# Sliding-window attention into a hard-swish product: unpadded casts, 64x64 transposes and one Q/K copy for batches 0 and 1

## The chip, the cores and the metric

The kernel runs on one core of a Trainium2 chip. The metric is device time of one execution in microseconds (us); of several runs the median is given. Engines: PE is TensorE (PEld its weight loads), DVE is VectorE, ACT is ScalarE, POOL is GpSimd, SP is SyncE, which issues the DMAs here.

## The reference

```
q, k, v: (8 batches, 8 heads, 576, 64); w_in (512, 2048); w_out (2048, 512); all float32
scores = (q @ k^T) / 8, kept where 0 <= i - j < 64, else -1e9
attn   = softmax(scores) ; o = attn @ v
x = o with heads side by side: (4608, 512)
h = x @ w_in ; g = h * clip(h + 3, 0, 6) / 6 ; out = g @ w_out
```

## The kernel before

**Tiling.** Attention goes by batch b and pair of heads g (0 to 3, two heads of 64 make 128 partitions). Its output, transposed, is xT. The second half goes by token block T of 512 tokens, nine of them: `s1(T)` (L620) multiplies xT with w_in (L641, 64 products of 512 columns a block, in most blocks each in two parts), ACT and DVE form g (L650, L653), and `s2(T)` (L661) multiplies with w_out (L685, 64 products), ACT copies the result out (L702) and SP stores it (L705). Attention of batch T+1 is placed between the L685 of `s2(T)`. Batch 0 comes ahead of everything.

**One pair of heads.** The scores of a 128-key block are needed for 192 queries only (QW). `scores` (L510) makes five key blocks for two heads: ten products (L530) on 64-row tiles of PE, one row half for each head. For batch 0 a product with a table of -30000 (L523) masks first; for later batches DVE multiplies by a 0/1 mask after the exponential (L550). ACT takes the exponential (L539, L545). `pv` (L558) is 18 products (L567, L572) with V, which has a column of ones for the sum; DVE divides (L582, L585). `xt` (L605) transposes the result on PE for batches 0 and 1 (L609) and ACT copies it to xT (L616); from batch 2 on a DMA transpose does (L592).

**Q and K.** From batch 2 on (`load_nat`, L362) POOL casts q and k to bf16, and one DMA transpose each (L371) makes QT and KT. For batches 0 and 1 (`load_pairs`, L296; `tq`, L486) a partition holds nine consecutive rows of one head. A load brings 64 partitions of one head and 64 of the other. Two casts of 64 partitions each write into a zero-padded tile (`padded`), with the second head in the upper columns. Nine products with `fold`, two 64x64 identities stacked (L500), give the transpose of one of Q and K for both heads, in f32. Two copies, 320 columns by DVE (L261) and 256 by ACT (L263), put rows back in order (L505). The copy and cast functions share the lines L261, L263 and L264 (one for each engine), so the profile tells them apart by tile name.

**Order.** All is put into order by a planner (`Plan`, L34) while the program is built: each engine's instructions come in the order of planned times. It holds a clock for PE (`pl.t`), booked costs for operations (`DUR`, `PER_COL`), a time for each engine's becoming free, and for DMA a running time `dma["t"]` that grows by kilobytes over a rate and lands 1.9 us later (`moved`, L253). The engine of each operation is fixed in tables (`ENG_CAST`, `ENG_TR`, L356). Batch 0's units are taken when `ready` (L459) says so, by `PRIO`. Batch 1's units are in the list `FIRST` (L748); at each L685 of `s2(0)` the head of the list is taken if the planner believes its inputs to have been ready for 0.3 us (L673). A unit placed too early holds everything behind it on PE.

Loads go out on SP in one sequence (`load_items`, L270): batch 0's q, k and V in two halves, w_in, w_out, batch 1's q and k, its V, then q, k and V of each later batch. Each load waits for a staging slot (`stage_slot`, six of them) and for its destination; the next one waits behind it.

```
                while side and side[0][0] <= n:
                    at_, f, b, g = side[0]
                    if b < NR6 and not ready(f, b, g):
                        break
```

Of the kernel before, what the change touches and what calls it, by code (L numbers as in the profile page):

```python
# [21 lines left out]
NQT = 1  # L22
NPT = 3
NNP = 4
NXP = 2
NEG = -30000.0
NWARM = 11
ENG_TR = ((("DVE", "ACT"), ("DVE", "ACT")), (("DVE", "ACT"), ("DVE", "ACT")))
DUR = lambda eng, n: {"DVE": 0.156 + 1.04e-3 * n, "ACT": 0.165 + 0.83e-3 * n}[eng]
PRIO = lambda g, f: ({"S": 0, "tq": 1, "tk": 1, "PV": 2, "X": 3}[f], g)  # L30
PAD_OF = ((0, 1, 0, 1), (2, 3, 0, 1))


class Plan:  # L34

# [20 lines left out]
    def pop(self):  # L56
        it = heapq.heappop(self.heap)
        ready, _, eng, dur, fn, key, then, deps = it
        for d in deps:
            if d not in self.done:  # L60
                self.parked.setdefault(d, []).append(it)
                return
            if self.done[d] > ready:
                heapq.heappush(self.heap, (self.done[d],) + it[1:])
                return
        start = max(ready, self.free.get(eng, 0.0))
# [32 lines left out]
def kernel(  # L99
# [18 lines left out]
    R = 9  # L118
# [48 lines left out]
    fold = consts.tile([P, NP], BF16, name="fold")  # L167
# [10 lines left out]
    padded = [[consts.tile([P, R, P], BF16, name=f"pad{i}{j}") for j in range(NNP)] for i in range(2)]  # L178
    natural = [consts.tile([P, NG, KB, P], BF16, name=f"nat{i}") for i in range(2)]
    QK_ring = [[consts.tile([P, NG, SP], BF16, name=f"{n}T{i}") for n in "QK"] for i in range(NQT)]  # L180
# [5 lines left out]
    for i in range(2):  # L186
        r = slice(i * NP, (i + 1) * NP)
        nc.vector.tensor_copy(out=fold[r, :], in_=ident32[r, r])
# [6 lines left out]

    for j in range(NNP):
        for i in range(2):
            for hf in range(2):
                r = slice((1 - hf) * NP, (2 - hf) * NP)
                eng, dur = "DVE", 0.3  # L200
                at(eng, (0.0, 0.0, 20.0, 20.0)[j], dur, zero(eng, padded[i][j][r, :, hf * D : (hf + 1) * D]),
                   ("pad", i, j) if hf else None)
    for pair in QK_ring:
        for t in pair:
            at("DVE", 4.5, 0.2, zero("DVE", t[:, :, S:SP]))
    at("DVE", 3.0, 0.25, lambda: nc.vector.tensor_copy(out=ident[:], in_=ident32[:]))
    at("DVE", 14.0, 0.06, lambda: nc.vector.memset(half[:], 0.5))
    for j, t in enumerate(P_ring):
        at("ACT", 1.9, 0.55, lambda t=t: nc.scalar.copy(
            out=t[:, :, 0 : KB - 1, QW : 2 * P], in_=idle[:].rearrange("p (h k w) -> p h k w", h=2, w=D)))  # L210
        at("ACT", 1.9, 0.4, lambda t=t: nc.scalar.copy(
            out=t[:, :, KB - 1, P : 2 * P], in_=idle[:, 0 : 2 * P].rearrange("p (h w) -> p h w", h=2)))

    def band(t, fill):
# [16 lines left out]
        out=neg[:, 2 * QW : TB], in_=neg32[:, 0:P]) and None, "neg", deps=("neg32",))  # L231
# [4 lines left out]
    ) and None, "mask", deps=("mask32",))  # L236
# [7 lines left out]
    dma = {"t": 2.0}  # L244
# [14 lines left out]
    def cast_op(eng, out_ap, in_ap):  # L259
        if eng == "DVE":  # L260
            return lambda s: nc.vector.tensor_copy(out=out_ap, in_=in_ap) and None  # L261
        if eng == "ACT":
# [3 lines left out]
    PER_COL = {"POOL": 0.83, "DVE": 0.45, "ACT": 0.83}  # L266
    ENG_CAST = ([(("DVE", "POOL"), ("ACT", "POOL"))] * 2 + [(("DVE", "POOL"), ("POOL", "POOL"))] * 2,
                [(("ACT", "POOL"), ("DVE", "POOL"))] * 4)
# [11 lines left out]
    def casts(key, land, pieces):  # L280
# [6 lines left out]
        for eng, o_ap, i_ap, cols in pieces:  # L287
            pl.op(eng, land, (0.3 if eng == "DVE" else 0.18) + PER_COL[eng] * cols / 1e3, cast_op(eng, o_ap, i_ap), None, one)

# [6 lines left out]
    def load_pairs(b):  # L296

        vs = load_v(b)
        for gg in range(0, NG, 2):
            tiles = {}  # L300
            deps = [stage_slot([("cast", b, i, gg), ("cast", b, i, gg + 1)]) for i in range(2)]
            for g in (gg, gg + 1):
                for i, src in enumerate((q, k)):
                    def go(s, g=g, i=i, src=src, tiles=tiles):
                        if i not in tiles:
# [6 lines left out]
                        fr, land = moved(s, 295, 380)  # L312
                        n = padded[i][PAD_OF[b][g]]
                        sv = st.rearrange("p (j d) -> p j d", j=R)
                        engs = ENG_CAST[b][g][i]
                        casts(("cast", b, i, g), land, [
                            (engs[1], n[NP:P, :, D:P], sv[NP:P], 576),
                            (engs[0], n[0:NP, :, 0:D], sv[0:NP], 576)])
                        return fr
                    before = [(bb, gg) for bb in range(b + 1) for gg in range(NG)  # L320
                              if (bb, gg) < (b, g) and PAD_OF[bb][gg] == PAD_OF[b][g]]
# [473 lines left out]
```

## Time and profile before

| | us |
|---|---|
| median of 11 runs | 320.22 |
| lowest and highest run | 319.14, 321.99 |
| the profiled execution | 319.55 |
| its span | 317.8 |
| PE busy | 300.2 |
| first L641 (w_in product of block 0) | 23.80 |
| first L641 of block 1 | 65.32 |

Times inside the profile count from the span's start. A line of a timeline has a start, a length, the engine, the line of the code, operation and tiles (written <- read), and how many in a row. "Idle before" names what ended the engine's wait. A matmul's length includes its way through the array, so a row of matmuls is read by their starts. The clock is the share of full speed that PE was granted.

### The profile page before, as it was taken

The numbers are of one execution on the slowest core, as the hardware profiler recorded it, in microseconds if no ns is written. First come the engines' busy times: TensorE is split into PE (matmuls) and PEld (weight loads), VectorE is DVE, ScalarE is ACT, GpSimd is POOL, SyncE is SP. The second block draws the span as 40 slices with busy tenths as digits, with TensorE's granted clock in tenths as the row PEclk, the third lists the DMA queues.
The fourth block names the chain that finished last, engine by engine and source line by source line (L and its number), as shares of the span: only waits on it lengthen the run. The fifth ranks groups of instructions, "written<-read, shape, count | busy, mean of one in ns | idle before, by whom it ended". The sixth has DMA issues, their size and how long they took to land.

```text
span 317.8 us, 5918 instructions
## 1 busy us (share of the span) xinstructions
PE 300.2 (94%) x2348; PEld 158.6 (50%) x2387; DVE 175.6 (55%) x216; ACT 174.9 (55%) x243; POOL 104.0 (33%) x153
## 2 busy tenths in 40 slices
PE   6769779999999999999999999999999999999995
PEld 2544345644454445785544454445575644444442
DVE  7686486637762676267717671777166717404610
ACT  5865368646834683368346833684368426315611
POOL 6787786622610265015601650067003000000000
PEclk9999979999999999999999999999999999999999
DMA  8999999999979899999999999999993430020011
GB/s 221 280 387 385 389 275 199 230 221 228 214 112 204 201 206 200 189 221 192 220 171 231 195 207 193 219 203 201 205 200 54 116 103 0 21 80 34 0 66 68
DMA packets 152812, 58.33 MB, mean 184 GB/s; under 512 B 142032, under 2 KB 142032, under 8 KB 152784
## 3 DMA queue, kind: packets, MB, share of 16 engines
q1 hardware_dynamic: 152784, 57.95, 83.0%
q8 instruction: 19, 0.31, 0.4%
q14 instruction: 9, 0.07, 0.1%
HBM read 36.70 MB, written 9.44 MB: 145 GB/s over the span
## 4 chain that ended last, share of the span: by engine, by line
PE 85%; DMA 8%; DVE 3%; ACT 1%; issue 1%; POOL 1%; POOLq 0%; ACTq 0%
PE acc L685 39%; PE ps L641 35%; DMA st<-in_moe_w_out_dram 5%; PE ps L530 4%; DMA st<-in_moe_w_in_dram 3%; PE ps L567 3%; PE ps L572 2%; PE ps L500 1%; DVE pad L261 1%; DVE pad L191 1%; POOL wout L264 1%; ACT pT L539 0%; POOL pad L264 0%; DVE gT L653 0%; PE ps L609 0%
## 5 line engine op out<-in xcount | busy, mean ns | idle before, releaser
L653 DVE SCALAR_TENSOR_TENSOR gT<-t,ps 128x1024 bf16<-128x1024 bf16 x72 | 87.9, 1221 | 94.2 <-ACT t L650 94.2
L685 PE MATMUL acc<-wout,gT 128*128 128x512 bf16 x551 | 132.5, 382 | 1.4 <-issue 0.3
L641 PE MATMUL ps<-xT,win 128*128 128x512 bf16 (+4 forms) x693 | 125.7, 340 | 0.7
L650 ACT ACTIVATE t<-ps,half 128x1024 bf16<-128x1024 f32 x72 | 80.2, 1114 | 47.5 <-PE ps L641 46.9
L641 PEld LDWEIGHTS <-win 128*128 128x128 bf16 x704 | 65.2, 98 | 59.8 <-issue 0.4
L685 PEld LDWEIGHTS <-gT 128*128 128x128 bf16 x576 | 53.1, 98 | 57.7 <-issue 0.5
L702 ACT COPY osb<-acc 128x512 f32<-128x512 f32 x36 | 21.2, 590 | 70.0 <-PE acc L685 68.8
L539 ACT ACTIVATE pT<-ps 128x768 bf16<-128x768 f32 x64 | 48.6, 817 | 10.1 <-PE ps L530 9.8
L264 POOL CAST V<-st 128x512 bf16<-128x512 f32 (+1 forms) x32 | 19.3, 606 | 103.3 <-DMA st<-in_v_dram 100.1
L264 POOL CAST nat<-st 128x512 bf16<-128x512 f32 x48 | 37.4, 783 | 20.4 <-DMA st<-in_q_dram 10.1
L550 DVE TENSOR_TENSOR pT<-pT,mask 128x1920 bf16<-128x1920 bf16 x28 | 35.3, 1261 | 8.0 <-ACT pT L545 8.0
L585 DVE TENSOR_TENSOR opg<-ps,rec 128x640 bf16<-128x640 f32 x32 | 26.4, 824 | 1.1
L567 PE MATMUL ps<-V,pT 128*128 128x65 bf16 x320 | 22.4, 194 | 3.4 <-ACT pT L539 2.0
L567 PEld LDWEIGHTS <-pT 128*128 128x128 bf16 x320 | 20.5, 98 | 9.1 <-ACT pT L539 2.5
L572 PE MATMUL ps<-V,pT 128*128 128x65 bf16 x256 | 21.3, 194 | 0.0
L530 PE MATMUL ps<-QT,KT 64*128 64x192 bf16 (+1 forms) x320 | 17.9, 239 | 1.0 <-ACT KT L263 0.4
L530 PEld LDWEIGHTS <-KT 64*128 64x128 bf16 x320 | 11.6, 94 | 14.0 <-issue 10.0
L572 PEld LDWEIGHTS <-pT 128*128 128x128 bf16 x256 | 17.9, 97 | 0.0
L582 DVE RECIPROCAL rec<-ps 128x10 f32<-128x10 f32 x32 | 6.9, 216 | 12.8 <-PE ps L572 12.8
L545 ACT ACTIVATE pT<-ps 128x256 bf16<-128x256 f32 x32 | 12.9, 402 | 0.0
L264 POOL CAST pad<-st 64x576 bf16<-64x576 f32 x18 | 11.6, 669 | 1.9 <-DMA st<-in_q_dram 1.2
L500 PE MATMUL ps<-fold,pad 128*128 128x64 bf16 x144 | 6.9, 200 | 5.3 <-POOL pad L264 3.3
(48 smaller groups left out, 102.8 us busy)
## 6 DMA issues: line engine op xcount, KB each, us to landing
out_dram<-osb SPq DMA_DIRECT2D x36, 256.0 KB, 2.7
st<-in_v_dram SPq DMA_DIRECT2D x28, 256.0 KB, 5.1
st<-in_q_dram SPq DMA_DIRECT2D x24, 256.0 KB, 5.3
st<-in_k_dram SPq DMA_DIRECT2D x24, 256.0 KB, 5.3
st<-in_moe_w_in_dram SPq DMA_DIRECT2D x4, 1024.0 KB, 9.9
st<-in_moe_w_out_dram SPq DMA_DIRECT2D x4, 1024.0 KB, 14.4
st<-in_q_dram SPq DMA_DIRECT2D x8, 288.0 KB, 6.2
st<-in_k_dram SPq DMA_DIRECT2D x8, 288.0 KB, 5.5
```

The lines of the kernel that those rows point to most:

```text
L264: return lambda s: nc.gpsimd.tensor_copy(out=out_ap, in_=in_ap) and None
L530: nc.tensor.matmul(st[:, h, off : off + w], lhsT=KT[h * D : (h + 1) * D, g, kb * P : (kb + 1) * P], rhs=QT[h * D : (h + 1) * D, g, kb * P ...
L539: nc.scalar.activation(out=pT[:, :, kbs[0] : kbs[0] + 2, 0:QW], in_=st[:, :, 0 : 2 * QW].rearrange("p h (k w) -> p h k w", k=2), func=EXP, ...
L550: pl.op("DVE", t, 1.2, lambda s: nc.vector.tensor_tensor(out=pT[:, :, :, 0:QW], in0=pT[:, :, :, 0:QW], in1=mask[:].rearrange("p (h k) w -> ...
L567: nc.tensor.matmul(ob, lhsT=pT[:, h, qb, 0:P], rhs=V[:, qb, 2 * g + h, :], start=True, stop=(qb == 0),)
L572: nc.tensor.matmul(ob, lhsT=pT[:, h, qb - 1, P : 2 * P], rhs=V[:, qb - 1, 2 * g + h, :], start=False, stop=True,)
L585: nc.vector.tensor_tensor(out=opg[:].rearrange("p k h d -> p h k d"), in0=ov[:, :, :, 0:D], in1=rec[:].unsqueeze(3).to_broadcast([P, 2, KB ...
L641: nc.tensor.matmul(hT[:, j, dst : dst + w], lhsT=win16[:, g, fc * P : (fc + 1) * P], rhs=xT[:, g, src : src + w], start=(g == 0), stop=(g ...
L650: nc.scalar.activation(out=t1[:], in_=hT[:], func=RELU, bias=half[:], scale=1.0 / 6.0)
L653: nc.vector.scalar_tensor_tensor(out=gT[:, 2 * c : 2 * c + 2, :], in0=cell["t"][:], scalar=1.0, in1=hT[:], op0=MIN, op1=MULT,)
L685: nc.tensor.matmul(accs[ts], lhsT=gT[:, fc, ts * P : (ts + 1) * P], rhs=wout16[:, fc, :], start=(fc == 0), stop=(fc == NFC - 1),)
L702: nc.scalar.copy(out=osb[:], in_=acc)
```

## The change

What it does, by parts:

- The zero-padded tiles, their memsets and `fold` go. Each load of q or k in batches 0 and 1 is cast whole (128 partitions, 576 columns) into a tile of its own, sixteen tiles.
- `tq` for Q and K becomes `tqk` for both: 36 bf16 transposes of 64x64, where the row half and column half of PE are set by the head, alternating between Q and K. The result is bf16. One copy of 1,152 columns puts both in order, on ACT or DVE.
- Q and K share one tile (`QK_tiles`); in batches 0 and 1 a pair's Q and K lie side by side.
- An operation may have several engines; the planner takes the one that would end first by its own figures (q and k casts of batches 0 and 1, V casts of batch 0, Q/K copies of batch 1, most x copies).
- The last key block's scores have 64 columns for 128, in all batches; what was beyond is set to 1 once, in the probabilities and in the mask.
- In batch 0 the scores of a pair become two units (S0, S1), and transposes no longer wait for the scores of the pair before.
- The loads of batch 2's V wait until both DMA transposes of batch 2 have been issued.
- Planner figures change: DMA start 2.4 for 2.0, rates 385, 200, 205 and 388 for 380, 220, 220 and 375.

```diff
-NNP = 4
+QK_ENG = ([('ACT',), ('DVE',), ('ACT',), ('DVE',)], (("DVE", "ACT"),) * 4)
+X_ENG = ([('DVE', 'ACT'), ('DVE', 'ACT'), ('ACT',), ('DVE',)], (("DVE", "ACT"),) * 4)
-PRIO = lambda g, f: ({"S": 0, "tq": 1, "tk": 1, "PV": 2, "X": 3}[f], g)
+PRIO = lambda g, f: ({"S0": 0, "S1": 0, "T": 1, "PV": 2, "X": 3}[f], g)
...
+        if isinstance(eng, dict):
+            pick = min(eng, key=lambda e: max(ready, self.free.get(e, 0.0)) + eng[e])
+            fn, dur, eng = fn(pick), eng[pick], pick
...
-    padded = [[consts.tile([P, R, P], BF16, name=f"pad{i}{j}") for j in range(NNP)] for i in range(2)]
+    runs = [[consts.tile([P, R, D], BF16, name=f"run{i}{j}") for j in range(NR6 * NG)] for i in range(2)]
-    QK_ring = [[consts.tile([P, NG, SP], BF16, name=f"{n}T{i}") for n in "QK"] for i in range(NQT)]
+    QK_tiles = [consts.tile([P, 2 * NG, SP], BF16, name=f"QKT{i}") for i in range(NQT)]
...
-    for j in range(NNP):
-        for i in range(2):
-            for hf in range(2):
-                r = slice((1 - hf) * NP, (2 - hf) * NP)
-                eng, dur = "DVE", 0.3
-                at(eng, (0.0, 0.0, 20.0, 20.0)[j], dur, zero(eng, padded[i][j][r, :, hf * D : (hf + 1) * D]),
-                   ("pad", i, j) if hf else None)
...
-        at("ACT", 1.9, 0.4, lambda t=t: nc.scalar.copy(
-            out=t[:, :, KB - 1, P : 2 * P], in_=idle[:, 0 : 2 * P].rearrange("p (h w) -> p h w", h=2)))
+        at("DVE", 2.0, 0.1, lambda t=t: nc.vector.memset(t[:, :, KB - 1, D:QW], 1.0))
...
+    def copy_op(kind, engs, n, ready, out_ap, in_ap, key, then=None):
+
+        cost = {e: COST[kind](e, n) for e in engs}
+        if len(cost) == 1:
+            eng = engs[0]
+            pl.op(eng, ready, cost[eng], cast_op(eng, out_ap, in_ap), key, then)
+        else:
+            pl.op(cost, ready, 0, lambda eng: cast_op(eng, out_ap, in_ap), key, then)
...
                         casts(("cast", b, i, g), land, [
-                            (engs[1], n[NP:P, :, D:P], sv[NP:P], 576),
-                            (engs[0], n[0:NP, :, 0:D], sv[0:NP], 576)])
+                            (("DVE", "ACT", "POOL"), runs[i][b * NG + g][:], st.rearrange("p (j d) -> p j d", j=R), R * D)])
...
+        if b == 2:
+            deps += (("issued", b, 1),)
...
+                    pl.mark(("issued", b, i), s)
...
-        if f in ("tq", "tk"):
-            ks = [("cast", b, int(f == "tk"), g)]
-            if b == 0 and g:
-                ks.append(("S", b, g - 1))
+        if f == "T":
+            ks = [("cast", b, i, g) for i in range(2)]
...
-    def tq(b, g, i):
+    def tqk(b, g):
+
+        for i in range(2):
             pl.wait(("cast", b, i, g))
+        tr = two_banks([("tr", b, g)], BF16)
+        for turn in range(2):
+            for j in range(R):
+                for i in range(2):
+                    h = slice((i ^ turn) * D, (i ^ turn) * D + D)
+                    nc.tensor.transpose(
+                        out=tr[h, i, j * NP : (j + 1) * NP], in_=runs[i][b * NG + g][h, j, :], identity=ident[h, h],
                     )
+        pl.pe(0.9)
+        copy_op(
+            "spread", QK_ENG[b][g], 2 * S, pl.t + 0.1,
+            QK_tiles[b % NQT][:, 2 * g : 2 * g + 2, 0:S].rearrange("d i (p j) -> d i p j", j=R),
+            tr[:, :, 0:S].rearrange("d i (j p) -> d i p j", p=NP), ("tr", b, g),
+        )
+        pl.mark(("T", b, g), pl.t)
...
-                w = min(QW, SP - kb * P)
+                w = min(QW, S - kb * P)
...
-                        out=pT[:, :, 4, 0:P], in_=st[:, :, 2 * QW : 2 * QW + P],
+                        out=pT[:, :, 4, 0:D], in_=st[:, :, 2 * QW : 2 * QW + D],
...
-        pl.op("ACT", pl.t + 0.1, 0.65, cast_op("ACT", xT[:, g, x0 : x0 + S], tr[:, 0:S]),
-              ("x", b, g))
+        copy_op("x", X_ENG[b][g], S, pl.t + 0.1, xT[:, g, x0 : x0 + S], tr[:, 0:S], ("x", b, g))
...
-        ("tq", 0), ("tk", 0), ("tq", 1), ("tk", 1), ("S", 0), ("tq", 2), ("tk", 2), ("S", 1), ("tq", 3),
-        ("tk", 3), ("S", 2), ("PV", 0), ("S", 3),
+        ("T", 0), ("T", 1), ("S", 0), ("T", 2), ("S", 1), ("T", 3), ("S", 2), ("PV", 0), ("S", 3),
```

## The prediction

> **What bounds the kernel now.** I read the page's totals and its forty slices first.
>
> ```profile
> PE 300.2 (94%) x2348; PEld 158.6 (50%) x2387; DVE 175.6 (55%) x216; ACT 174.9 (55%) x243; POOL 104.0 (33%) x153
> PE   6769779999999999999999999999999999999995
> PEclk9999979999999999999999999999999999999999
> ```
>
> A slice is 7.9 us. From the eighth slice on TensorE (PE) is full; before it there are holes, and in the sixth (40 to 48 us) the granted clock falls. The change touches batches 0 and 1, which lie in those holes; behind 65.3 us it can give only what shortens PE's own work. Next, the chain that ended last, and PE's timeline beside it (start, us, what):
>
> ```profile
> 13.82 10.36 DMA st<-in_moe_w_in_dram
> 24.18 14.31 DMA st<-in_moe_w_out_dram
> 38.55 0.73 POOL wout L264
> ...
> 39.53 1.05 POOL wout L264
> ...
> 40.63 0.68 POOL pad L264
> ...
> 41.35 0.44 PE ps L500 x9
> ```
>
> ```profile
> 23.80 14.22 PE L641 MATMUL ps<-xT,win 128*128 128x512 bf16 x62
> ```
>
> PE ends the first product of token block 0 (L641) at 38.02. The next instructions in program order are batch 1's first transposes (L500). They need a half cast that sits on GpSimd (POOL) behind two casts of w_out: weights land at 38.5, w_out is cast until 40.6, then the pad, 41.35 PE goes on. The windows of 2 us (PE busy, PEld, DVE, ACT, POOL, clock, DMA share, GB/s) show the price:
>
> ```profile
> 38.00:40.00 2.00, 0.01 (x1) 0.00 (x0) 0.00 (x0) 0.74 (x2) 1.46 (x2) 1.00 1.06 392
> 40.00:42.00 2.00, 0.65 (x11) 0.42 (x12) 1.78 (x2) 2.00 (x3) 1.94 (x4) 0.93 1.06 393
> 42.00:44.00 2.00, 2.00 (x14) 1.04 (x13) 1.71 (x5) 1.23 (x3) 2.00 (x4) 0.50 1.20 293
> ```
>
> 3.3 us idle, and then 3.4 us at half clock, which lose another 1.7: 5.0 us, the largest loss outside steady work. DMA runs at 390 GB/s from 16 to 42 us, so when weights and batch 1's q and k land (first q 39.26, first k 40.01, by what ACT and DVE wait for) is fixed by bytes; the change moves no byte there.
>
> Why does the code put a transpose there? The planner's own clock (I add up its figures; they give the order only) ends that product at 41.02 where the trace says 38.02, and takes batch 1's first casts as ready at 40.94. It believes that nothing waits.
>
> **The change part by part.**
>
> *Casts and zero padding.* Gone are sixteen DVE memsets of 298 ns; the first eight (1.8 to 4.9 us) hold up DVE's first pad cast until 5.87. Thirty-two half casts (18 on POOL at 669 ns, 8 on DVE at 730, 6 on ACT at 663; 21.4 us in all) become 16 casts of 576 columns on all partitions, each at the same 0.66 to 0.73 us or less, since an operation costs by columns: about 11 us. Only batch 0's first one, and batch 1's first pair, are on the path. The POOL cast that PE waits for at 40.63 can go to a free engine: the k cast, landed at 40.01, then ends at about 40.7 on ACT.
>
> *One copy for Q and K.* Sixteen DVE copies of 320 columns (0.485) and sixteen of 256 on ACT (0.457), 15.1 us, become eight of 1,152. On ACT the exponentials give the slope: 256 columns 392 ns, 768 columns 808, so 1,152 cost 1.12 us; on DVE between 1.2 and 1.36 us. Less engine time, but a later first score by 0.2 to 0.4 us a pair, where both engines shared the work. In batch 1 w_out products cover it (0.216 us each; the chain shows 49 in 10.74 us); in batch 0 the next pair's transposes lie beside it.
>
> *Transposes.* The one part that makes PE work longer. Rows of before:
>
> ```profile
> 48.48 0.43 PE L500 MATMUL ps<-fold,pad 128*128 128x64 bf16 x9
> 48.74 0.81 PE L685 MATMUL acc<-wout,gT 128*128 128x512 bf16 x3
> ...
> 111.19 1.03 PE L685 MATMUL acc<-wout,gT 128*128 128x512 bf16 x4
> 112.15 0.56 PE L530 MATMUL ps<-QT,KT 64*128 64x192 bf16 x10
> 112.64 1.04 PE L685 MATMUL acc<-wout,gT 128*128 128x512 bf16 x4
> ```
>
> Nine 64-column products with their weight loads take 0.26 us, 29 ns each; a pair of heads needs 18, 0.53 us. The new form has 36. The scores (L530) show what half-array tiles cost: the four L685 end at 111.19 + 4 x 0.216 = 112.05, scores start 0.10 later, and their five pairs of 0.38 us end in a gap of 0.10: 0.19 us for changing the tile shape and back. No row shows 64x64 tiles. Bounds: two tiles side by side, 18 x 29 ns + 0.19 = 0.72 us; one after another at today's pace, 36 x 29 + 0.19 = 1.24.
>
> A rule speaks against this: the Trainium skill, TensorEngine Tiling (Array Packing), "Tile-to-Partition Mapping", Restrictions, says that column tiling switches the fast weight load off, and TensorE: Matmul & The Clock Gate, "LDWEIGHTS", prices a plain load at columns / 1.2 ns, 53 ns for 64. Today's row (128-column loads every 29 ns) is the fast kind and can't refute it. By the rule an estimate is 18 x 53 + 0.19 = 1.15 us if the two tiles overlap as the scores' do, and 36 x 53 + 0.19 = 2.1 if not. I take 1.24, nearest the row and close to the rule's overlapping case: 0.7 us more a pair, 2.8 us for batch 1. Batch 0's pay the same, largely inside its waits.
>
> The same page ("Part 4: PE-mode transpose") says that transposes don't count as activity for the clock, so replacing true products by them could leave batch 0 at half clock: up to 5 us, if its 3.2 us of PE's queue a pair doubled and L641 started near 31. The trace speaks against that: from 20 to 24 us PE does one pair's PV (0.5 us) and ten transposes, and the clock stays 1.00. I take nothing.
>
> *Scores.* The last key block has 64 columns for 128. The last pair takes 56 ns now (0.38 less four of 82) and 29 then: 27 ns for each of the 24 score blocks behind 65 us, where PE is full: -0.65 us. ACT saves 0.1 us in each, off the path. In batch 0 the block is split in two with its own mask product, one more shape change, +0.19 a pair inside waits.
>
> *x copies to DVE or ACT.* 0.64 us on ACT; hidden in batch 1. The last of batch 0 ends 0.85 us after PE's first L641, so some 0.2 to 0.4 us may come off there; counted in the next step.
>
> *Where batch 0 ends.* Walking through with these durations, first transposes at 5.3 (6.70 before), then PE's own queue of 1.2 + 1.45 + 0.55 us a pair and ACT's exponentials, L641 starts at about 22.4 instead of 23.8 and ends at 36.6. The floor is 21.4, the end of w_in's first cast. If batch 0 gained nothing, 38.0.
>
> *Where the wait goes.* Now T(1,0). In the new planner's sums, first q lands at 2.4 + 8 x 295/385 + 1179/200 + 8 x 1049/388 + 295/385 + 1.9 = 38.7 (start, batch 0's q and k, its V, the weights, q itself, landing), k at 39.5, the cast ends at 40.2, ready at 40.5; its product ends at about 37.6. So about (40.5 - 37.6) / 0.216 = 14 w_out products go ahead of T(1,0). On the chip they run from 36.6 to 39.6, and the transposes start at 40.75, when k is cast. 1.1 us of idle stay, too short for the clock to fall, as only the 3.3 us did so. An earlier or slightly later end of L641 changes little: the landing of k decides.
>
> Behind 40.75: 50 products 10.8, four transposes T, four scores at 0.56 (2.2), PV and x transposes 4 x (0.56 + 0.28) = 3.4, and 0.4 of small gaps: 57.5 + 4T. T = 1.24 gives 62.5, against 65.3 in the trace. The same sum for before (41.35 + 13.8 + 2.1 + 2.4 + 3.4 + 1.7 cold + 0.6 gaps) is 65.3. V of batch 1 doesn't bind: cast by 51.6, and PV(1,3), x and copy some 7 us later.
>
> *Batch 2's V behind its transposes.* Five loads and five POOL casts of 0.61 move behind the transpose of K on SP (issued 66.82, 4.5 us there); what V stood ahead of, K's issue and one store, gets earlier, what is behind it, batch 3's q, keeps its place as the sum of transfers is the same. V would be cast near 78 as now (77.9); PV(2,0) comes at 85.0, at 82 then. Worth nothing while PE leads no more than some 6 us; without the cover it would cost its lateness once. K landed at 73.3, scores at 79.9; later batches show 4 to 7 us of such slack, so a shift of 3 us carries to the end.
>
> Sum: 62.5 - 65.3 = -2.8, and -0.65: -3.5 us. The profiled run, 319.55 us with its span of 317.8, becomes 316.1. It lies 0.7 below the median of the runs, 320.22; against that median, 316.8.
>
> **The rivals.**
>
> 1. *Likeliest: partial removal*, 316.8. Chance 0.47.
> 2. *More falls away.* T costs 0.72 and the planner's n is higher, so that no idle time stays: 57.5 + 2.9 - 1.1 = 59.3; just above V's chain at 58.6. Minus 6.0 and 0.65: 313.6; half of it, 315. The scores' tiles, which do overlap, speak for it, the weight-load rule against. Chance 0.21.
> 3. *The wait stays.* If the planner puts T(1,0) after five products or fewer, PE idles 3 us again with a cold window: 40.75 + 12.7 + 1.7 + 5.0 + 6.0 = 66.2, +0.9 - 0.65: 320.4. The order is then changed in name only. Its clock's past error of 3 us speaks for this, my sum of 14 against. Chance 0.14.
> 4. *Slower: the tiles serialize.* If a 64x64 weight load neither overlaps its neighbour nor its own product, each of 36 costs 53 + 27 = 80 ns, T = 3.1: batch 1 alone gives 57.5 + 12.3 = 69.8, +4.5 - 0.65: 324.0. The balance lies where 57.5 + 4T - 0.65 = 65.3, T = 2.1, 53 ns a transpose. Against it: score tiles start in pairs. Chance 0.18.
>
> **How the numbers follow.** About 0.3% is what this measurement can tell from no change, so faster is below 319.3 and slower above 321.2. Cases 1 and 2 are faster, with some of case 1 (T near 1.9) within: 0.66. Case 3 is mostly within: 0.16. Case 4 is slower: 0.18. The range goes from 314.2 (most of case 2) to 321.6 (case 3 and the mild end of 4).
>
> **What would show it.** Right: L641 starts by 22.5; L685 stand ahead of batch 1's first transposes; PE's idle time there is about 1 us; no clock of 0.50 at 42 to 45; 36 transposes from first start to the next L685 in 1.2 us; L641 of block 1 starts near 62.5; scores blocks 27 ns shorter; the rest shifted as a whole. Wrong: transposes spaced over 50 ns, a cold window, PE waiting for KT or V in batches 2 and 3, or ACT or DVE held by a cast that waits for its DMA.

## The result and the profile after

The changed kernel takes 317.41 us, the median of 13 runs (316.47 to 318.92), beside 319.59 for the kernel before (50 runs in all, 319.07 to 322.12). The ratio is 0.993, 95% interval 0.9914 to 0.9947. The profiled execution took 316.47 us with a span of 314.8, against 319.55 and 317.8: 3.1 us less; forecast for it were 316.1. It is the fastest of the 13 runs. In the medians 2.2 us are saved, where the forecast had 3.4: 316.8 against 320.22, the median of the 11 runs of the front table, which are among the 50. One execution below, the profiled one of units_at_once, ran at half pace (631.34 us) and is left out of its median and ratio. The totals and the two slice rows of the changed kernel's page:

```profile
PE 301.4 (96%) x2494; PEld 158.9 (50%) x2531; DVE 172.0 (55%) x201; ACT 165.3 (53%) x220; POOL 94.5 (30%) x133
PE   6889979999999999999999999999999999999994
PEclk9999979999999999999999999999999999999999
```

DVE, ACT and POOL lose 3.6, 9.6 and 9.5 us of busy time, PE gains 1.2. The clock row looks as before: its one weak slice, the sixth, has not gone. PE's timeline shows what lies there (in the changed kernel the batch 0/1 transposes are L497, scores L528, w_in products L638, w_out products L682):

```profile
21.89 14.04 PE L638 MATMUL ps<-xT,win 128*128 128x512 bf16 x62
35.76 2.48 PE L682 MATMUL acc<-wout,gT 128*128 128x512 bf16 x10
38.63 1.02 PE L682 MATMUL acc<-wout,gT 128*128 128x512 bf16 x4 [0.39 <-POOL wout L261]
40.68 0.21 PE L497 MATMUL ps<-ident,run 64*64 64x64 bf16 x1 [1.02 <-DVE run L258]
41.46 0.84 PE L497 MATMUL ps<-ident,run 64*64 64x64 bf16 x35 [0.57 <-ACT run L260]
42.63 0.63 PE L682 MATMUL acc<-wout,gT 128*128 128x512 bf16 x1 [0.33 <-issue]
...
62.32 4.91 PE L638 MATMUL ps<-xT,win 128*128 128x512 bf16 x21
```

Block 0's w_in products start 1.91 us earlier than before and end 2.3 us earlier, at 35.76, where the first w_out product starts. Fourteen w_out products now stand where PE only waited. Then PE waits for batch 1's q (DVE's cast), does one transpose, and waits again for k (ACT's cast). The chain names the end of that wait, and the 2 us windows its price:

```profile
30.50 10.21 DMA st<-in_k_dram
...
40.74 0.68 ACT run L260
...
41.46 0.84 PE ps L497 x35
```

```profile
38.00:40.00 2.00, 1.26 (x6) 0.29 (x3) 0.01 (x1) 0.00 (x0) 1.31 (x2) 1.00 1.05 391
40.00:42.00 2.00, 0.75 (x33) 0.64 (x35) 2.00 (x3) 0.67 (x1) 1.52 (x2) 0.99 1.06 394
42.00:44.00 2.00, 1.67 (x44) 1.10 (x41) 1.26 (x4) 1.12 (x1) 0.00 (x0) 0.50 1.13 345
```

The wait is no longer for a cast on POOL but for the bytes of k themselves, and DMA moves 391 to 394 GB/s in it. But k is later than the forecast had it, and the reason lies far ahead. The windows from 12 to 18 us, first of before, then of after (the last column is GB/s):

```profile
12.00:14.00 2.00, 1.77 (x34) 1.29 (x34) 2.00 (x4) 1.33 (x2) 1.88 (x3) 1.00 1.34 236
14.00:16.00 2.00, 1.35 (x25) 0.94 (x27) 0.74 (x5) 1.90 (x6) 1.62 (x4) 1.00 0.98 263
16.00:18.00 2.00, 1.58 (x33) 1.19 (x31) 1.69 (x4) 1.72 (x4) 1.83 (x6) 1.00 1.05 387
```

```profile
12.00:14.00 2.00, 1.53 (x55) 1.25 (x55) 1.05 (x3) 1.74 (x3) 0.89 (x2) 1.00 1.19 252
14.00:16.00 2.00, 1.50 (x42) 0.98 (x43) 1.67 (x4) 0.78 (x3) 1.61 (x5) 1.00 0.66 131
16.00:18.00 2.00, 2.00 (x21) 0.82 (x19) 1.78 (x3) 1.93 (x4) 1.80 (x5) 1.00 1.04 400
```

SP's issues of the w_in loads, of before (L415) and after (L419), fit that:

```profile
12.56 2.50 SPq L415 DMA_DIRECT2D st<-in_moe_w_in_dram  x4
```

```profile
13.58 2.71 SPq L419 DMA_DIRECT2D st<-in_moe_w_in_dram  x4
```

The first load of w_in is issued 1.0 us later, the transfers have a hole of 132 GB/s x 2 us = 0.26 MB at 14 to 16 us, and at 391 GB/s those bytes are 0.7 us: k's cast starts at 40.74 where k was there at 40.01. The bytes moved up to 38 us, summed from both traces, agree: 12.52 MB before, 12.24 after.

And the clock still falls to 0.50 from 41.98 to 45.39. Block 1 begins at 62.32, against 65.16 before (the front table's 65.32 is where the chain takes up that line; its first product starts at 65.16). From there on blocks follow each other after 32.21, 32.22 and 32.37 us before, and after 32.11, 32.10 and 32.27 in the changed kernel: 0.1 us less for each block that has an attention unit beside it. The last product starts 3.35 us earlier (310.45 for 313.80). The span shrinks by only 3.0, since the tail behind the start of the last product is 4.3 us for 4.0.

### The profile page after: what moved, and what is told of

Read it like the earlier page. It is cut to its first block, busy times and chain, and to the rows that moved or that the text cites. A ratio compares the mean times of both kernels' runs of the same rounds, so it can differ in the third digit from the quotient of the medians.

```text
span 314.8 us, 6130 instructions
## 1 busy us (share of the span) xinstructions
PE 301.4 (96%) x2494; PEld 158.9 (50%) x2531; DVE 172.0 (55%) x201; ACT 165.3 (53%) x220; POOL 94.5 (30%) x133
## 4 chain that ended last, share of the span: by engine, by line
PE 85%; DMA 9%; SPq 3%; issue 1%; POOL 1%; ACT 0%; ACTq 0%
PE acc L682 39%; PE ps L638 35%; PE ps L528 4%; DMA st<-in_moe_w_in_dram 4%; DMA st<-in_k_dram 3%; PE ps L565 3%; PE ps L570 2%; DMA st<-in_v_dram 2%; SPq L354 1%; SPq L316 1%; PE ps L497 1%; POOL win L261 1%; PE ps L607 0%; ACT run L260 0%; ACT osb L699 0%
## 5 line engine op out<-in xcount | busy, mean ns | idle before, releaser
L682 PE MATMUL acc<-wout,gT 128*128 128x512 bf16 x550 | 132.0, 380 | 2.4 <-issue 1.0
L638 PE MATMUL ps<-xT,win 128*128 128x512 bf16 (+4 forms) x693 | 125.7, 340 | 0.6
L638 PEld LDWEIGHTS <-win 128*128 128x128 bf16 x704 | 65.3, 98 | 59.8 <-issue 0.2
L682 PEld LDWEIGHTS <-gT 128*128 128x128 bf16 x576 | 52.9, 98 | 58.4 <-issue 1.0
L261 POOL CAST V<-st 128x512 bf16<-128x512 f32 (+1 forms) x30 | 18.0, 601 | 110.5 <-DMA st<-in_v_dram 85.6
L261 POOL CAST nat<-st 128x512 bf16<-128x512 f32 x48 | 38.5, 808 | 20.0 <-DMA st<-in_k_dram 11.7
L565 PE MATMUL ps<-V,pT 128*128 128x65 bf16 x320 | 21.9, 194 | 0.3 <-issue 0.3
L570 PE MATMUL ps<-V,pT 128*128 128x65 bf16 x256 | 20.9, 193 | 0.0
L528 PEld LDWEIGHTS <-QKT 64*128 64x128 bf16 x320 | 11.6, 95 | 14.7 <-issue 11.5
L528 PE MATMUL ps<-QKT 64*128 64x192 bf16 (+1 forms) x320 | 18.0, 237 | 0.0
L261 POOL CAST nat<-tl 64x512 bf16<-64x512 f32 x12 | 10.3, 861 | 2.2 <-DMA tl<-in_k_dram 1.1
L497 PE MATMUL ps<-ident,run 64*64 64x64 bf16 x288 | 7.2, 201 | 3.9 <-DVE run L258 2.4
L258 DVE CAST run<-st 128x576 bf16<-128x576 f32 x13 | 6.1, 472 | 7.6 <-DMA st<-in_q_dram 5.8
```

Source lines behind the costliest of these rows:

```text
L261: return lambda s: nc.gpsimd.tensor_copy(out=out_ap, in_=in_ap) and None
L528: nc.tensor.matmul(st[:, h, off : off + w], lhsT=KT[h * D : (h + 1) * D, kb * P : (kb + 1) * P], rhs=QT[h * D : (h + 1) * D, kb * P : kb * ...
L565: nc.tensor.matmul(ob, lhsT=pT[:, h, qb, 0:P], rhs=V[:, qb, 2 * g + h, :], start=True, stop=(qb == 0),)
L570: nc.tensor.matmul(ob, lhsT=pT[:, h, qb - 1, P : 2 * P], rhs=V[:, qb - 1, 2 * g + h, :], start=False, stop=True,)
L638: nc.tensor.matmul(hT[:, j, dst : dst + w], lhsT=win16[:, g, fc * P : (fc + 1) * P], rhs=xT[:, g, src : src + w], start=(g == 0), stop=(g ...
L682: nc.tensor.matmul(accs[ts], lhsT=gT[:, fc, ts * P : (ts + 1) * P], rhs=wout16[:, fc, :], start=(fc == 0), stop=(fc == NFC - 1),)
```

## The experiments

Each ratio is to the kernel before on the same chip. The first four experiments ran on one chip, the next four on a second, the last four on a third. "Block 1" is the start of its first w_in product, in the profile. Three add work of their own on PE (fill_mm, fill_tr, late_batch0).

| run | median, us | ratio, 95% interval | block 0, block 1, us |
|---|---|---|---|
| fill_mm | 317.31 | 0.9912 [0.9878, 0.9945] | 22.44, 61.66 |
| fill_tr | 317.53 | 0.9896 [0.9866, 0.9926] | 21.98, 61.51 |
| hold24 | 316.79 | 0.9880 [0.9852, 0.9907] | 23.09, 62.61 |
| tile_runs | 318.94 | 0.9943 [0.9916, 0.9971] | 24.48, 63.12 |
| after_same_chip | 318.18 | 0.9950 [0.9927, 0.9974] | 24.38, 62.62 |
| before_move | 320.62 | 1.0018 [0.9994, 1.0042] | 23.96, 63.77 |
| late_batch0 | 317.91 | 0.9945 [0.9921, 0.9969] | 24.16, 63.95 |
| v_not_held | 317.41 | 0.9924 [0.9897, 0.9952] | 22.06, 63.63 |
| units_at_once | 320.74 | 1.0027 [1.0010, 1.0043] | none |
| hold24_v | 317.97 | 0.9935 [0.9911, 0.9958] | 24.19, 62.43 |
| hold24_again | 317.03 | 0.9915 [0.9886, 0.9944] | 23.37, 61.45 |
| after_third_chip | 317.72 | 0.9937 [0.9916, 0.9958] | 24.28, 62.48 |

### Is the cold window the idle time's doing, and do transposes count?

Two kernels fill the wait ahead of batch 1's first transposes, one with five products of zeros, one with twenty 128x128 transposes of the identity; nothing reads the results. In `tqk`, for batch 1's first pair:

```
+        if (b, g) == (1, 0):
+            pad = two_banks(["fill"])
+            for _ in range(5):
+                nc.tensor.matmul(pad[:, 0, :], lhsT=idle[:, 0:P], rhs=idle[:], start=True, stop=True)
+            pl.mark("fill", pl.t)
```

```
+            pad = two_banks(["fill"], BF16)
+            for _ in range(20):
+                nc.tensor.transpose(out=pad[:, 0, 0:P], in_=ident[:], identity=ident[:])
```

> The changed kernel with five products on zeros (512 columns, 1.1 us) put on PE just ahead of batch 1's first transposes, where PE idles from 39.3 to 40.7; nothing else is moved. Theory A, the clock fell at 42 us because PE was idle for too much of the 3.4 us before: with the filler the clock stays 1.00 from 42 to 45, block 1's first w_in product comes at 60.6 instead of 62.3 (-1.7), and the time falls by about 1.7 to near 315.7. Rival B, the clock falls because of the 64x64 transposes themselves, which run in that window: the clock still drops to 0.50, and the time stays within 0.5 us of the changed kernel.

> As the run before, but the filler is twenty 128x128 transposes of the identity (56 ns each, 1.1 us too) instead of five products. Theory A1, any work of PE counts for the clock: as with products, clock 1.00 from 42 to 45 and about -1.7 us. Theory A2, transposes don't count as activity: the clock falls to 0.50 as in the changed kernel and the time stays where it was, within 0.5 us.

The windows of the kernel with added transposes, and one of the kernel with added products:

```profile
38.00:40.00 2.00, 1.57 (x9) 0.69 (x9) 0.00 (x0) 0.00 (x0) 1.31 (x2) 1.00 1.05 392
40.00:42.00 2.00, 1.45 (x30) 1.24 (x29) 1.62 (x2) 0.67 (x1) 1.91 (x2) 1.00 1.05 391
42.00:44.00 2.00, 1.84 (x73) 1.42 (x70) 1.43 (x4) 1.17 (x2) 0.00 (x0) 1.00 1.11 349
```

```profile
42.00:44.00 2.00, 1.84 (x73) 1.49 (x74) 1.50 (x4) 1.12 (x1) 0.00 (x0) 1.00 1.08 369
```

The clock stays at 1.00 in both profiles. The clock's windows (last section) begin at nearly the same time in the three, 38.55 and 38.68 us in the fills and 38.56 in the changed kernel, so it isn't their place that differs. Over all runs, the mean clock is 0.999 or more in 7 of the fills' 13 and in 3 of the changed kernel's 34. So the idle time did cost a cold window, and transposes hold the clock as products do. The prediction had weighed the Trainium skill's sentence in "TensorE: Matmul & The Clock Gate", "Part 4: PE-mode transpose", that a transpose doesn't count as PE-busy the way a product does, and took nothing for it; this run contradicts the sentence.

The price of the window reads best from the start of the 35 transposes that k releases (41.46 to 42.9 in the executions, since k lands at different times) to block 1: 62.32 - 41.46 = 20.86 us with the cold window; 61.66 - 41.92 = 19.74 and 61.51 - 41.85 = 19.66 without; 62.48 - 42.66 = 19.82 in after_third_chip, where the clock is warm there too. The window costs 1.0 to 1.2 us. Both expectations had 1.7, half of 3.413 us; but the columns that PE worked in it are 0.37 of what it holds at full clock, 1.26 us, and half clock adds that much at most. In medians the two fills can't be told from the changed kernel with certainty: they stand at 0.9912 and 0.9896, the changed kernel at 0.993 to 0.995, and the intervals overlap except for fill_tr against after_same_chip, which were measured on different chips.

### Do the two 64x64 tiles work side by side?

The same 36 transposes, in runs of nine, eighteen and nine on one tile instead of alternating:

```
-        for turn in range(2):
-            for j in range(R):
-                for i in range(2):
-                    h = slice((i ^ turn) * D, (i ^ turn) * D + D)
+        for i in range(2):
+            for turn in range(2):
+                h = slice((i ^ turn) * D, (i ^ turn) * D + D)
+                for j in range(R):
```

> The changed kernel with the same 36 transposes of a pair in another order: nine in a row on one 64x64 tile, then nine on the next, instead of alternating between two tiles. Theory D, the 0.56 us of a block come from two tiles that work side by side: a block then takes 36 x 29 ns = 1.05 us or more[...], which adds at least 4 x 0.5 = 2 us in batch 1 where PE is full: about +2 us, to 319.5[...]. Rival E, PE's issue of 72 instructions sets the 0.56 us whatever their tiles: no difference, within 0.5 us.

PE's timeline for batch 1's second pair and the next product, here and then in after_third_chip, where the clock is equally warm:

```profile
43.89 1.12 PE L497 MATMUL ps<-ident,run 64*64 64x64 bf16 x36
44.94 0.39 PE L682 MATMUL acc<-wout,gT 128*128 128x512 bf16 x1
```

```profile
43.88 0.85 PE L497 MATMUL ps<-ident,run 64*64 64x64 bf16 x36
44.65 0.39 PE L682 MATMUL acc<-wout,gT 128*128 128x512 bf16 x1
```

First start to next product: 1.05 us in runs, 0.77 alternated. From first to last start 36 take 0.929 us in runs, and 0.562 alternated in the next two pairs of after_third_chip (0.653 in this one, whose second start comes 0.09 us late). The single starts say why. In runs they follow each other after 31 or 32 ns within a tile; only where the tile changes do some stand 5 ns apart. Alternated, two start 3 or 4 ns apart and the next two 28 or 29 ns later, 32 ns for two. So two tiles run side by side, and one tile alone needs 32 ns for a load with its product, not the 53 ns that the prediction's estimate took from the Trainium skill's load ("TensorE: Matmul & The Clock Gate", "LDWEIGHTS"). Rival E, that PE's issue sets the pace whatever the tiles, falls. The 0.28 us of this pair and 0.37 of the next make some 1.3 us for batch 1's four, not the 2 expected, and in the ratios they can't be told (0.9943, and 0.9950 for the changed kernel on another chip).

### Does the new order carry the gain, or the cheaper casts and copies?

Both halves of that question have a run. before_move is the kernel before with only its order changed: batch 1's units start at the 17th w_out product. units_at_once is the changed kernel with its first transposes taken at once, as before.

```
-    FIRST = [(0, f, g) for f, g in (
+    FIRST = [(16, f, g) for f, g in (
```

```
-                if b < NR6 and not ready(f, b, g):
+                if b < NR6 and (f, g) != ("T", 0) and not ready(f, b, g):
```

> The kernel before, with only one thing altered: batch 1's units are allowed from the 17th w_out product of block 0 on (index 16 for 0), so that its first transposes come at about 38.0 + 16 x 0.216 = 41.5, when the pad cast that they waited for is done. Theory A, most of what the change gained is the place of those transposes, not the casts, copies or tiles: no idle of 3.3 us, no cold window, block 1's first w_in product at 60.2 to 61.5 instead of 65.2, and the time 3.5 to 5 us below the kernel before, at or below the changed kernel. Rival F, the unpadded casts and the single copies carry the gain: moving the place alone gives less than 1.5 us, as the pad casts on ACT and DVE hold up batch 1 anyway.

> The changed kernel in which batch 1's first transposes are taken at the first w_out product, without asking the planner whether their inputs are there: casts, transposes and copies of the change, in the order that the kernel before had. Theory A (the gain at batch 1 needs the new order, the cheaper casts and copies give none by themselves): w_in products of block 0 end near 35.8 us as in the changed kernel, PE then idles until k is cast, 4.9 us up to 40.7, with a cold window behind it, and the 14 products of 3.0 us come later instead: block 1 starts at 62.3 + 3.0 = 65.3, the kernel is 3 us slower than the changed one, ratio to the kernel before 0.998 to 1.003. Rival B (the casts and copies carry the gain, the order is only where it shows): block 1 starts below 63.5, ratio 0.997 or less.

PE's timeline of before_move:

```profile
39.31 3.62 PE L685 MATMUL acc<-wout,gT 128*128 128x512 bf16 x16
42.76 0.69 PE L500 MATMUL ps<-fold,pad 128*128 128x64 bf16 x18
44.23 0.42 PE L500 MATMUL ps<-fold,pad 128*128 128x64 bf16 x9 [0.78 <-DVE gT L653]
44.49 0.38 PE L685 MATMUL acc<-wout,gT 128*128 128x512 bf16 x1
46.58 0.42 PE L500 MATMUL ps<-fold,pad 128*128 128x64 bf16 x9 [1.71 <-ACT QT L263]
```

The wait ahead of the first transposes is gone, and two others stand behind it: 0.78 us for DVE (L653) and 1.71 us for ACT's half copy (L263). DVE is late for both: two padded casts stand ahead of its own half copies, and ACT's copy waits 1.42 us for the first of these:

```profile
44.10 1.55 DVE L261 CAST pad<-st 64x576 bf16<-64x576 f32 x2
45.58 0.47 DVE L261 CAST QT<-ps 128x320 bf16<-128x320 f32 x1
46.08 0.45 ACT L263 CAST QT<-ps 128x256 bf16<-128x256 f32 x1 [1.42 <-DVE QT L261]
```

In the median the new order alone is worth nothing (1.0018). The profiled run is no typical one: it is the second fastest of twelve (318.15 us), and block 1 starts in it 1.4 us earlier than in the kernel before. Its mean clock shows one cold window; that of eight others shows two (0.988 or 0.989, where one window of 3.413 us makes 0.995). Where the second lies wasn't profiled, so what takes the gain in a typical run is shown only in part.

The new casts and copies in the old order are worth nothing either: 1.0027, and its eleven clocks are 0.984 to 0.989, two or three cold windows, although the shorter scores are in it as well. Its one profile can't be read beside the others, so the 4.9 us wait itself wasn't seen. Together the two runs say that the 0.7% needs both parts, the order and the cheaper casts and copies. That the order takes the wait away is shown; that the casts and copies are worth so much because they keep other waits from standing in its place is what before_move's profile suggests.

### Is batch 0's earlier end worth anything?

Four more products of zeros ahead of batch 0 make it start and end later:

```
+    for i in range(4):
+        nc.tensor.matmul(warm[:, 0, :], lhsT=idle[:, 0:P], rhs=idle[:], start=True, stop=True)
```

> The changed kernel with four more products on zeros (0.43 us each, 1.7 us) at PE's start, which the planner isn't told of, so that the order stays and batch 0 runs later. Theory A, batch 1's first transposes wait for the landing of k, so a later batch 0 only eats idle time: the first w_in product moves from 21.9 to about 23.3, the products before the transposes end at about 40.5, the transposes still come at about 41.5, PE idles 1 us instead of 2.2, the clock stays 1.00, and the time is the same or about 1 us less than the changed kernel on this chip. Rival G, batch 0's end sets the time: +1.4 us.

> The changed kernel unaltered, so that the others of this call have it on the same chip: 0.993 of the kernel before, within 0.3%.

Both are the same in the median, 0.9945 and 0.9950: the added products cost nothing that can be told. As a test of a later block 0 it is weaker than it was meant, for after_same_chip starts block 0 as late by itself (24.38 for 24.16; the first profile of the changed kernel has 21.89), and in each of the late ones k lands late as well. The profiles fall into an early and a late group:

| execution | first w_in load issued | k's first cast starts | block 0, block 1, us |
|---|---|---|---|
| before | 12.56 | 40.01 (k there) | 23.80, 65.16 |
| after | 13.58 | 40.74 | 21.89, 62.32 |
| fill_tr | 13.71 | 41.13 | 21.98, 61.51 |
| fill_mm | 14.08 | 41.20 | 22.44, 61.66 |
| after_third_chip | 14.59 | 41.93 | 24.28, 62.48 |
| late_batch0 | 14.58 | 42.20 | 24.16, 63.95 |
| after_same_chip | 14.73 | 42.14 | 24.38, 62.62 |

A microsecond at w_in's first issue is about a microsecond at k, also in the profiles not listed (13.62 us with 40.84, 13.72 with 40.72, 14.43 with 41.57, 14.80 with 41.99 and 42.05); no run moved that issue on purpose. In the late group the clock has its cold window in batch 0 (in hold24_again, an early one, too), and the hole in the transfers is deep. In after_third_chip:

```profile
14.00:16.00 2.00, 0.73 (x33) 0.62 (x35) 0.90 (x3) 0.19 (x2) 1.80 (x4) 1.00 0.42 73
16.00:18.00 2.00, 2.00 (x23) 0.59 (x15) 2.00 (x3) 1.13 (x3) 1.83 (x5) 0.50 0.83 251
```

PE, DVE and ACT all have little to do from 14 to 16 us there, and the clock falls behind it. PE waits for POOL's casts of batch 0's last q and k. They start as these land, at 13.93 and 14.76 us, a microsecond later than in the changed kernel's first profile (12.91 and 13.78):

```profile
PE ps L497 <- POOL run L261: 1.7, 2, 1.1
```

Yet block 1 starts at nearly the same time in after (62.32: k early, cold window at 42) and in after_third_chip (62.48: k 1.2 us later, no cold window left). So block 0's start, 2.4 us apart, doesn't set block 1's; k's landing and the one cold window do, and in some executions V: late_batch0's 63.95 holds a wait of 1.26 us of the first PV for POOL's last cast of batch 1's V, which ends at 54.4 there and at 52.8 in after.

### Is the hold on batch 2's V worth anything?

```
-        if b == 2:
-            deps += (("issued", b, 1),)
```

> The changed kernel without the wait of batch 2's V loads for the issue of batch 2's DMA transposes. Theory A, the wait is worth nothing: K of batch 2 lands 2 to 5 us later on SP, by 73 to 75, still ahead of its scores at 77.1; the same time within 0.5 us. Rival H, with PE 3 us earlier than in the kernel before, K is now late without it: PE waits at 77 us and the time is 1 us or more longer.

The ratio is 0.9924 [0.9897, 0.9952] without the hold, 0.9950 [0.9927, 0.9974] with it: no loss, as forecast; no worth of this part can be told. Its profile's late block 1 (63.63) comes from a wait of 1.31 us for batch 1's V, as in late_batch0, and from a cold window at 41.2.

### Can the remaining wait go?

Holding batch 1's units back to the 25th w_out product puts ten more products into the wait; hold24_v lets batch 1's V casts go to DVE or ACT as well.

```
-    FIRST = [(0, f, g) for f, g in (
+    FIRST = [(24, f, g) for f, g in (
```

```
-                    eng = ("DVE", "ACT", "POOL") if b == 0 else ("POOL",)
+                    eng = ("DVE", "ACT", "POOL") if b < NR6 else ("POOL",)
```

> The changed kernel, with batch 1's units allowed only from the 25th w_out product of block 0 on (the list's index 24 for 0), so that batch 1's first transposes stand behind 24 products, not 14, and both casts have landed when PE comes to them. Theory A, the wait of 2.2 us and the cold window are all that is left to gain there: no idle time, no cold window, block 1's first w_in product near 58.6 to 59.5, where batch 1's V (cast near 51.6, and 7 us of attention behind it) becomes the limit; the time falls by 2.8 to 3.7 us, to about 314. Rival C, the order is bound elsewhere (V or the copies): the gain is under 1.5 us, with new waits of PE behind 50 us.

> The kernel with batch 1's units held back to the 25th w_out product once more, beside the other three on one chip. If its lead over the changed kernel is real, its ratio to the kernel before stays 0.004 or more below that of the changed kernel in this set. If the lead was chance of the chip, the two agree within 0.002.

> The changed kernel with batch 1's units held back to the 25th w_out product, and in addition batch 1's five V casts free to go to DVE or ACT as well. In the run with the units held back, PE waited 1.3 us for GpSimd's last V cast, of a half tile that landed at 52.04 and took 1.24 us there. Theory A (that cast's engine sets the end of the wait): the last V cast ends near 52.7 on another engine, the wait falls to about 0.7 us, and the kernel is 0.6 us faster than the one with the units held back, ratio to the kernel before 0.985 to 0.988. Rival B (a V cast on ACT or DVE stands ahead of the exponentials or copies that PE needs, and waits there for its DMA): no gain, or a loss of up to 1 us, and PE's waits name ACT or DVE at 45 to 55 us.

> The changed kernel itself, for the other three to be set against on one chip. Ratio to the kernel before 0.991 to 0.996, block 1 at 62 to 62.7 us where no clock window is cold or one is. If block 1 starts a microsecond earlier in a profile without a cold window at 42 us, the cold window's price is about 1.2 us rather than the 1.7 of the prediction.

With hold24 the waits among the first transposes fall to 0.25 us, and PE's waits from 36 to 66 us in hold24_again show where it goes:

```profile
PE ps L565 <- POOL V L261: 1.1, 1, 1.1
PE acc L682 <- ACT osb L699: 0.5, 1, 0.5
```

The next floor is V's landing and cast; hold24's block 1 (62.61) misses the 58.6 to 59.5 of its expectation, and so does its time the 314. From the end of block 0's w_in products to block 1 pass 26.56 us in the changed kernel's first profile, 24.33 in after_third_chip, 25.65 in hold24 and 24.21 in hold24_again. The medians favour hold24: 0.9880 and 0.9915, the changed kernel 0.993, 0.9950 and 0.9937. On the one chip where both ran, 0.9915 [0.9886, 0.9944] and 0.9937 [0.9916, 0.9958] overlap, and the difference of 0.002 lies between what the two expectations asked for. By these medians it is the fastest version tried, but its lead over the changed kernel isn't certain.

Spreading V's casts takes the wait for V away and brings two others, from 36 to 66 us:

```profile
PE ps L497 <- DVE QKT L258: 0.6, 1, 0.6
PE acc L682 <- ACT osb L699: 0.5, 1, 0.5
PE ps L528 <- ACT pT L543: 0.5, 1, 0.5
```

DVE does a V cast at 48.10, and its copy of Q and K, which PE needs, starts at 48.45 behind it. The rival held; 0.9935 is no gain.

## Why the prediction was right, and where some of its terms were wrong

- **The wait and its place: right.** Block 0's w_in products started at 21.89 (forecast 22.4) and ended at 35.76 (36.6). Fourteen products went ahead of T(1,0), as the planner's sum had said. They ended near 39.5 (39.6). The early start of block 0 is not safe: in the other two profiles of this kernel it is 24.38 and 24.28, later than before (23.80).
- **The landing of k, "fixed by bytes; the change moves no byte there": 0.7 us off.** The 35 transposes started at 41.46 for 40.75. k's cast started when the sum had it end, since the loads of w_in, far ahead of it, were issued 1.0 us later than before. In other executions it is up to 1.5 us later still.
- **"1.1 us of idle stay, too short for the clock to fall": failed.** The idle time was 1.02 + 0.57 us with one transpose between, and the clock fell. The prediction asked for one idle stretch; what decided was the work within a fixed window of 3.413 us, 38.56 to 41.98, in which both waits lie: products and transposes filled 0.38 of it. It cost 1.0 to 1.2 us (the fills).
- **T, "1.24, nearest the row": mis-sized by 0.4 us a pair.** The four pairs of after_third_chip take 0.91, 0.77, 0.69 and 0.91 us from first start to next product, 3.3 for 5.0, near the lower bound of 0.72. That is 1.7 us to the good. 29 ns serial is about what one tile alone takes (32), but the kernel alternates; the scores' overlapping half tiles were the nearest row, and the prediction had named them.
- **The errors cancelled, by luck.** With the measured transposes the prediction's own sum, 57.5 + 4T, is 20.0 us from k's transposes to block 1 (counted from 40.75), and the warm profiles show 19.66 to 19.82: its other terms hold within 0.4. Then 40.75 + 20.0, +0.7 for k, +1.1 for the cold window, is 62.6, against 62.5 forecast and 62.32 measured.
- **Scores: right.** -0.65 us forecast. Five of the six blocks concerned follow 0.10 to 0.12 us sooner, the sixth 0.03 later in this profile (32.40 us, 32.27 in most other executions): -0.5 in all. The last product starts 2.84 + 0.51 = 3.35 us earlier, of -3.5 forecast.
- **Casts, copies and x copies off the path: right in that they cost nothing, wrong in what they are for.** The prediction put nearly the whole gain down to the order. before_move shows that the order without them gains nothing in the median.
- **"V of batch 1 doesn't bind": only just.** Forecast was a cast by 51.6; it ended at 52.8, when the first PV had begun (52.50), with no wait in that profile and 1.3 us in three of the experiments' profiles. The prediction had compared it with the last PV, 7 us later, where the first one needs all of V.
- **Batch 2's V: right,** no worth can be told (v_not_held). K of batch 2 landed at 74.47 us in the trace of before, not at 73.3, so its slack was 5.4 us.
- **The rivals.** "The wait stays" fell by the fourteen products, but its cold window came; "the tiles serialize" fell at 16 ns a transpose. "More falls away" was right in T and wrong in the idle time. The cold window took back 1.1 of the 1.7 us that T gave, and k's later landing 0.7.
- **The medians: two thirds of the forecast.** The sum was made for a profiled run, and the one it met is the fastest of its 13. In the medians 2.2 us came of 3.4.

Still open: what makes SP issue w_in's first load a microsecond later than before, and another microsecond later in some executions. In the first profile half of the microsecond comes with the last load of the first half of batch 0's V (2.03 us for 1.53), half with the first four loads of its second half (2.65 for 2.09); in after_third_chip the last V load ahead of w_in takes 3.28 us to issue, for 1.91 in the first profile and 1.95 before. The traces name nothing that these issues wait for, and no run took one of them apart. Open too is how much of the spread of the changed kernel's runs (316.5 to 318.9), and so of the missing third, this makes, and how much the cold windows and the late x transposes of the last section.

## What to carry to other kernels

A planner's order and the cost of what it orders are one change: a reordering that removes a wait shows its gain only if the engines behind it can follow, so ask for each moved step who is late next. In a stage fed by transfers, check when each load can be issued as well as its bytes, and sum PE's work over windows of the clock's length, 3.413 us here, instead of measuring the longest idle stretch. Where tiles of a new shape have no row, take the row of the shape that overlaps in the same way, and not that of the same instruction in the old shape.

## What the runs showed of the hardware that was not expected

**The clock follows the work in a window.** Every cold stretch between the kernel's start and its tail lasts 3.413 us, and its grid lies elsewhere in each execution. With a column at 0.42 ns (a product of 512 columns each 0.216 us; one on a tile of 64 rows counts half) the share of a window that PE worked can be added up from the records. It says what the clock does next:

| run, window from us | products + transposes, share | clock in the next window |
|---|---|---|
| before, 38.31 | 0.13 + 0 | 0.50 |
| after, 38.56 | 0.25 + 0.13 | 0.50 |
| after_third_chip, 12.57 | 0.14 + 0.16 | 0.50 |
| after_third_chip, 5.74 | 0.14 + 0.28 | 1.00 |
| hold24_again, 11.83 | 0.19 + 0.20 | 0.50 |
| fill_mm, 38.55 | 0.56 + 0.01 | 1.00 |
| fill_tr, 38.68 | 0.25 + 0.37, of that 0.31 added | 1.00 |

Other windows stayed warm at 0.33 (before_move, 44.11 us) and 0.34 (fill_mm, 4.41), so the line lies between 0.33 and 0.4 and isn't sharp in this sum. The two windows of after_third_chip differ, to two digits, in their transposes alone. In batch 0 the new, shorter work is thin enough that some executions lose a window there, as the grid falls.

**Blocks are now close to x's DMA transposes.** Some blocks of the changed kernels take 32.5 to 33.4 us instead of 32.11; PE then waits at the first product of a block for x's transpose, here in hold24_again:

```profile
PE ps L638 <- DMA xT<-opg: 0.9, 1, 0.9
```

The two first profiles, before and after, show no such wait; fill_mm has 1.3 us of it, after_same_chip 0.3. What delays that transpose in some executions wasn't tried.
